# Longer DRAM rows for the prepared weights, and a reordered hand-over between the stages, in a fused attention, max-of-three and SoLU layer-norm kernel

## The chip, the cores and the metric

The kernel runs on one core of a Trainium2 chip. The metric is device time in microseconds (us) of one execution; before the change the median of three runs is 717.21 us.

## The reference

Everything is float32, and one launch computes three layers one behind the other:

```python
# attention: q, k, v are (4, 12, 448, 64)
scores = matmul(q, k.T) / 8 - log(448);  attn = 1 / (1 + exp(-scores));  y = matmul(attn, v)
x = y as (1792, 768)
# max of three: w1, w2, w3, w_out are (768, 768)
h = max(max(x @ w1, x @ w2), x @ w3);    x = h @ w_out
# SoLU layer norm: w_in (768, 1024), w_out (1024, 768)
h = x @ w_in
e = exp(h - max(h));  solu = h * e / sum(e)
ln = (solu - mean(solu)) / sqrt(var(solu) + 1e-6) * g_ln
out = ln @ w_out
```

## The kernel before

Each float32 matrix product is three TensorE products of operands split into a high and a low part (high by high, high by low, low by high). The two layers behind attention use a fast 2x2 block scheme: seven products P1 to P7 instead of eight, whose operands are sums and differences of blocks. The two products `h @ w_out` and `@ w_in` have no step between them, so their weights are multiplied together on the chip; the seven block operands of the result are B11, B21, T2, T1, T3, T4, B22, which is the order `LOADS`.

**Attention (0 to 205 us)** takes 24 pairs of heads (`scores` L250, `attend` L271, `take_x`). Beside it the raw weights are loaded on POOL's queue (L140) and split (`prepare`), the weight product runs (L469), and its seven operands are cast, high and low, and written to DRAM tensors `w_d` on SP's queue (L485).

**Units (205 to 478 us).** Eighteen units are 9 weight groups by 2 token halves `bp`; the last two are `bp` = 1, then `bp` = 0. A unit has seven products of 9 matmuls of 448 columns (L638), in PE's order: its P1; P4 and P3 of the unit before; its P2, P6, P5, P7. ACT copies X out of PSUM three times a unit (`held`, L678: e1, u2, u3) since the next product overwrites it. `sums` takes the maximum over three units into tiles `hs` (FIN[0..3] for the first half, FIN[4..7] for the second) and writes them to DRAM, `h_d` (L668). Meanwhile `convert_w2` splits the last layer's weights on ACT and DVE and writes 64 pieces to `w2_d`.

**Stage L (to 561 us)** multiplies h by the prepared weights for seven pairs of 128-token tiles, p = 0 to 6, second half first: nine matmuls of 512 columns a product (L894). Weights `wf` come from `w_d` by seven loads on POOL's queue (`load_wf` L724). Blocks `a` come back from `h_d` (`load_h` L699, on SP); of the first pair the last 128 rows come from `hs` directly (`last_rows` L708). `prep_l(p)` makes a pair's operands out of them: casts on ACT (L51), sums and low parts on DVE (L59, L56). After a pair, `solu_ln` (L932 and on) normalises it on ACT and DVE, transposes it and writes it to DRAM (`u_d`).

**Stage O (to the end)** does the same with the normalised rows: seven pairs, twelve matmuls of 384 columns a product; weights `w2t` come by 28 loads on POOL (`load_w2` L730), into slots that stage L's last pair gives up one by one (`release`), blocks `ut` from `u_d` (`load_u`), operands from `prep_o`.

What sets the order: PE, ACT and DVE run in the order in which the Python code issues. In the stages L and O `pace`, called after every matmul, hands out steps of two queues, `bg` (operand preparation) and `lazy` (normalising), for the time that the matmul earned; a product whose operands are not yet issued forces `bg` steps until they are (`product_c`). Operands lie in a ring of ten slots (stage L one each, stage O two); `bg` stops while the slot ten places back is unread. POOL's order is that of the code from stage L on. SP's order is left to the scheduler, and on SP a DMA waits until the one eight issues before it has landed.

```python
turn_of["n"] += 1                                   # pace, L881 on
first, second = (bg, lazy) if turn_of["n"] % 2 else (lazy, bg)
```

Of the kernel before, what the change touches and what calls it, by code (L numbers as in the profile page):

```python
# [44 lines left out]
def sigmoid_attention_max_moe_solu_ln(tc, q, k, v, w123, wo, wi, w2, g, out):  # L45
# [37 lines left out]
    raw_cm, rawp = open_pool("rawp", RAWS, side="right")  # L83
    st_cm, stp = open_pool("stp", 2, side="right")
    xa_cm, xa = open_pool("xa", 1, side="right")
    wi_cm, wip = open_pool("wip", 1, side="right")
    ws_cm, wsp = open_pool("wsp", 2, side="right")
    f_cm, fpool = open_pool("fpool", 1)
    a_cm, apool = open_pool("apool", 2)
    ps1 = [open_pool("ps_sc", 3, space=PSUM), open_pool("ps_av", 2, space=PSUM)]  # L90
# [5 lines left out]
    dve.memset(warm, 0.0)  # L96
    pool.memset(bias_s, -math.log(S))

    w_d = {nm: dram.tile([P, 3, 2, 528], F32, name=f"w_d{nm}") for nm in LOADS}
    w2_d = [dram.tile([4, P, 2 * len(nms), HU], F32, name=f"w2_d{n}") for n, nms in enumerate(PIECES)]  # L100
    h_d = [dram.tile([3, P, NT], F32, name=f"h_d{k}") for k in range(2)]
    u_d = [dram.tile([4, 32, 4, 256], F32, name=f"u_d{t}") for t in range(TT)]


# [295 lines left out]
    def convert_w2(key):  # L400
        _, kc, j = key
        y, z = words(key)
        scale(y, key)
        yield
        upper(y)
        yield
        lower(y, key)
        yield
        for i in range(2):
            half = y[:, i * QU : (i + 1) * QU]  # L410
            act.activation(half, half, AF.Copy, scale=g_sb[:, kc + 4 * i : kc + 4 * i + 1])
        yield
        tt(z[:, :QU], y[:, OU : OU + QU], y[:, :QU], ALU.subtract)
        yield
        tt(z[:, QU : QU + OU], y[:, QU : QU + OU], z[:, :OU], ALU.subtract)
        tt(z[:, QU + OU :], y[:, QU + OU :], z[:, QU : QU + OU], ALU.subtract)
        yield
        for n, src in enumerate((y[:, QU:], z[:, :QU], z[:, QU:], y[:, :OU])):
            w = OU * len(PIECES[n])
            if n == 3:  # L420
                t = stp.tile([P, QU], F32, tag="stg1", name=f"w2s{kc}_{j}_{n}", bufs=1)
            else:
                t = staging(f"w2s{kc}_{j}_{n}")[:, : 2 * w]
            hi, lo = (t[:, i * w : (i + 1) * w].bitcast(F32R) for i in range(2))
            copy(act, hi, src)
            yield
            rest(dve, lo, src, hi)
            if n == 3:
                done(key)
            sp.dma_start(  # L430
                out=w2_d[n][kc, :, :, j * OU : (j + 1) * OU], in_=t.rearrange("p (m c) -> p m c", c=OU)
            )
            yield

# [21 lines left out]
    def gen_w(fc, n):  # L456
        if fc == FC - 1:
            ps = ps_av.tile([P, 512], F32, tag="av", name=f"pw{n}_{fc}")
        else:
            if n == 0:  # L460
                pws[fc] = ps_sc.tile([P, 2, 512], F32, tag="sc", name=f"pw{fc}")
            ps = pws[fc][:, n]
        i = 0
        for kc in range(KC):
            wt = slots[("wo", fc, kc // 3)]
            cols = slice((kc % 3) * P, (kc % 3 + 1) * P)
            c0 = (n * KC + kc) * 512
            for a, b in ((0, 0), (0, 1), (1, 0)):
                pe.matmul(  # L469
                    ps, lhsT=wt[:, a, cols], rhs=wi_t[:, b, c0 : c0 + 512], start=(i == 0), stop=(i == 3 * KC - 1)  # L470
                )
                i += 1
                if i % 2 == 0:
                    run_bg()
        c = fc // 2

        def temp(k):
            return wsp.tile([P, 512], F32, tag=f"t{k}", name=f"wt{k}_{c}", bufs=1)

        def put(nm, src):  # L480
            t = wsp.tile([P, 2, 512], F32R, tag="ws", name=f"ws{nm}_{c}", bufs=4)
            copy(act, t[:, 0], src)
            yield
            rest(dve, t[:, 1], src, t[:, 0])
            sp.dma_start(out=w_d[nm][:, c, :, :512], in_=t.bitcast(F32))  # L485
            yield

        def now(gen):
            for _ in gen:
                pass  # L490

        if fc % 2 == 0:
            if n == 1:
                b11, b12 = (pws[fc][:, m] for m in range(2))
                wts[1], wts[3] = temp(1), temp(3)
                now(put("B11", b11))
                copy(act, wts[3], b12)
                tt(wts[1], wts[3], b11, ALU.subtract)
                bg.appendleft(put("T1", wts[1]))
            return  # L500
        if fc == FC - 1 and n == 0:
            wts[2] = temp(2)
            copy(act, wts[2], ps)
            bg.appendleft(put("B21", wts[2]))
        elif n == 1:
            t1, t3 = wts[1], wts[3]
            tt(t1, ps, t1, ALU.subtract)
            tt(t3, ps, t3, ALU.subtract)
            now(put("B22", ps))
            if fc < FC - 1:  # L510
                b21 = pws[fc][:, 0]
                now(put("B21", b21))
                wts[2] = temp(2)
            else:
                b21 = wts[2]
            tt(wts[2], b21, t1, ALU.subtract)
            bg.extendleft(put(nm, wts[k]) for nm, k in (("T4", 2), ("T3", 3), ("T2", 1)))
# [13 lines left out]
        slots.pop(("wo", fc, 0))  # L531
        slots.pop(("wo", fc, 1))
    run_bg(1 << 20)
    shut(ws_cm, wi_cm)
    xat_cm, xat = open_pool("xat", 1, side="right")
    x_tiles(0, xat, TS)
    xb_cm, xb = open_pool("xb", 1, side="right")
    x_tiles(1, xb, BS)

# [106 lines left out]
    def sums(u, i, j, ps, add):  # L646

        gi, bp = u
        fp, w = divmod(gi, 3)
        b = 2 * bp + j  # L650
        if (i, b) not in hs:
            nm, n = FIN[len(hs)]
            while (1, nm, n) in fts:
                run_bg()
            hs[(i, b)] = f_tile(nm, n, f"hs{i}_{b}")
        h = hs[(i, b)]
        if w == 0:
            if add is None:
                act.copy(h, ps)
            else:  # L660
                tt(h, ps, add, ALU.add)
        elif add is None:
            tt(h, ps, h, ALU.max)
        else:
            tt(add, ps, add, ALU.add)
            tt(h, add, h, ALU.max)
        if w == 2:
            sp.dma_start(out=h_d[i][fp, :, b * S : (b + 1) * S], in_=h)  # L668

    def held(u, nm, ps):  # L670
        k = state["e"] % 5
# [14 lines left out]

    def h_tile(p, i, k):
        if p % 2:
            t = f_tile(*FIN[i + 2 * k], f"a{p}_{i}{k}")[:, :HU]
        else:  # L690
            t = afirst.tile([P, HU], F32, tag=f"a{i}{k}", name=f"a{p}_{i}{k}")
        hts[(p, i, k)] = t
        return t.rearrange("p (f t) -> p f t", f=3)

    def load_h(p, k, rows=slice(0, 3)):

        for i in range(2):
            t = tiles[2 * p + i]
            sp.dma_start(  # L699
                out=h_tile(p, i, k)[:, rows], in_=h_d[k][rows, :, t * P : (t + 1) * P].rearrange("f p t -> p f t")  # L700
            )

    def last_rows(k):

        for i in range(2):
            t = tiles[i]
            b, c0 = divmod(t * P, S)
            sp.dma_start(out=hts[(0, i, k)][:, 2 * P :], in_=hs[(k, b)][:, c0 : c0 + P])  # L708

    units = [(gi, bp if gi < NG - 1 else 1 - bp) for gi in range(NG) for bp in range(2)]  # L710
    bg.extend(split_t(1, nm, i) for nm, i in FIN)
# [9 lines left out]

    def load_wf(nm, tag):
        t = wfs[("L", nm)] = wslot[tag].tile([P, 3, 2, 512], F32R, tag=f"s{tag}", name=f"wf{nm}")
        pool.dma_start(out=t.bitcast(F32), in_=w_d[nm][:, :, :, :512])  # L724

    def load_w2(nm, tag):
        t = wfs[("O", nm)] = wslot[tag].tile([P, 4, 2, HU], F32R, tag=f"s{tag}", name=f"w2t{nm}")
        n, off, w = next((n, nms.index(nm), len(nms)) for n, nms in enumerate(PIECES) if nm in nms)
        for kc in range(4):
            pool.dma_start(out=t[:, kc].bitcast(F32), in_=w2_d[n][kc][:, off::w])  # L730

    def clear(i):
        at = wops.get(("at", i))
# [76 lines left out]
    for n, u in enumerate(units):  # L810
# [8 lines left out]
        if old is not None:  # L819
# [4 lines left out]
            if old["u"] == (NG - 1, 1):  # L824
# [4 lines left out]
                for tag in (2, 3, 4):  # L829
                    load_wf(LOADS[tag], tag)  # L830
                last_rows(1)
                bg.append(prep_l(0))
        Z = ps_z.tile([P, 512], F32, tag="z", name=f"z{n}")[:, :S]
        product(Z, u, "P2", True, True)
        sums(u, 0, 0, Z, e1)
        product(X, u, "P6", False, False)
        u2 = held(u, "u2", X)
        V = ps_v.tile([P, 512], F32, tag="v", name=f"v{n}")[:, :S]
        product(V, u, "P5", True, False)
        product(X, u, "P7", False, False)  # L840
# [30 lines left out]
            return True  # L871
        return False

    turn_of = {"n": 0}

    def pace(dt):
        credit["t"] += dt
        while credit["t"] > 0:
            turn_of["n"] += 1
            first, second = (bg, lazy) if turn_of["n"] % 2 else (lazy, bg)  # L880
            if not step(first) and not step(second):  # L881
                credit["t"] = 0.0

    def product_c(ps, kind, p, name, start, stop):
# [98 lines left out]
        s1 = tp.tile([P, 4, P], F32, tag="s1", name=f"os1_{p}", bufs=1).rearrange("p k (i t) -> p k i t", i=4)  # L983
        return prep("O", p, *a, s1, lambda t: t.rearrange("p (k i t) -> p k i t", k=4, i=4), 0.69)

    spare = [("e", None)] * 3 + FIN[4:8] + FIN[10:]

    def block(name):
        nm, i = spare[state["e"] % len(spare)]
# [53 lines left out]
    for n, (kind, p) in enumerate(stage):  # L1043
# [20 lines left out]
            close(old)  # L1064
        if n == 1:
            load_w2(LOADS[0], 7)
        if n + 1 < NP2:
            load_h(p + 1, 0)
            load_h(p + 1, 1)
        elif n + 1 < len(stage):  # L1070
            load_u(n + 1 - NP2)
        if kind == "L":
            new_st(p)
# [90 lines left out]
```

## Time and profile before

| | |
|---|---|
| three runs, us | 717.21, 714.24, 721.55 (median 717.21) |
| profiled execution | 716.61 us, span 714.8 us |
| PE (TensorE) busy | 659.2 us, 92% of the span |
| PEld (weight loads) | 529.2 us |
| DVE (VectorE) busy | 489.8 us, 69% |
| ACT (ScalarE) busy | 372.4 us, 52% |
| POOL (GpSimd) busy | 69.3 us |
| DMA | 125.43 MB, mean 175 GB/s |
| mean granted TensorE clock | 0.964 |

Times in the rows below are from the start of the span; "busy" counts executing instructions. PEclk is the granted clock as a share of 2.4 GHz, whose lower level is 1.2 GHz. In a row of the timeline `[3.48 <-DMA wfT<-w_dT]` means that the engine was idle for 3.48 us just before, and that a DMA writing `wfT` from `w_dT` ended it; "issue" there means that no wait in the records explains the time. q0 is the queue of DMAs that POOL issues, q1 that of SP and ACT.

### The profile page before, as it was taken

What the parts mean: (1) busy time and instruction counts of PE and PEld (TensorE: products, weight loads), DVE (VectorE), ACT (ScalarE), POOL (GpSimd) and SP (SyncE); (2) the same over time, 40 slices, a digit from 0 to 9 for tenths busy, and PEclk for the clock granted to TensorE, in tenths of its full rate; (3) what the DMA queues carried; (4) which work ended last, traced back from release to release, by engine and by line L of the source; (5) the groups of instructions that cost most, each with busy time, mean ns of one, the idle gap of its engine ahead of it and who ended that gap; (6) DMA issues with size and microseconds to landing.
All of it is one profiled execution on the core that took longest, in us unless ns stands there. A gap on an engine that the chain in (4) does not pass through costs nothing.

```text
span 714.8 us, 9650 instructions
## 1 busy us (share of the span) xinstructions
PE 659.2 (92%) x3283; PEld 529.2 (74%) x3283; DVE 489.8 (69%) x1057; ACT 372.4 (52%) x709; POOL 69.3 (10%) x121
## 2 busy tenths in 40 slices
PE   9999999899999999999999993879988977797997
PEld 6555687545579999999999992658766665787997
DVE  4799977697477888778886854248766753565752
ACT  5888334578665455454455422127655533376341
POOL 1111110001001011101101001010000333000000
PEclk9999999999999999999999996879999997799999
DMA  8678688736202556646665377883511699343421
GB/s 301 205 259 249 181 282 307 270 104 220 76 1 70 140 173 224 165 135 171 189 199 150 84 219 243 282 316 96 159 55 61 209 282 286 101 145 102 154 85 67
DMA packets 87009, 125.43 MB, mean 175 GB/s; under 512 B 35632, under 2 KB 63664, under 8 KB 86960
## 3 DMA queue, kind: packets, MB, share of 16 engines
q1 hardware_dynamic: 74608, 71.10, 31.2%
q0 software_dynamic: 12208, 53.48, 24.4%
q8 instruction: 26, 0.43, 0.2%
q14 instruction: 23, 0.19, 0.1%
q10 hardware_dynamic: 144, 0.23, 0.1%
HBM read 84.15 MB, written 40.37 MB: 174 GB/s over the span
## 4 chain that ended last, share of the span: by engine, by line
PE 66%; DVE 12%; DMA 8%; issue 7%; ACT 4%; POOL 2%; SPq 0%; DVEq 0%; ACTq 0%; POOLq 0%
PE x L638 18%; PE X L894 12%; PE v L638 8%; PE av L271 7%; PE V L894 6%; PE z L638 4%; PE sc L250 4%; PE Z L894 3%; DMA h_d<-hs 3%; PE sc L246 2%; POOL w2tT L730 2%; DMA a<-h_d 1%; DMA a<-hs 1%; DVE y_wo L156 1%; DVE wt L59 1%
## 5 line engine op out<-in xcount | busy, mean ns | idle before, releaser
L271 PE MATMUL av<-sf,vr 128*64 128x448 f32 x384 | 77.5, 545 | 0.0
L258 ACT ACTIVATE sf<-sc,bias_s 128x896 f32<-128x896 f32 x72 | 67.7, 1010 | 1.5 <-PE sc L250 0.3
L250 PE MATMUL sc<-qt,kt 64*128 64x448 f32 x432 | 52.3, 378 | 4.9 <-ACT sf L255 4.9
L271 PEld LDWEIGHTS av<-sf,vr 128*64 128x64 f32 x384 | 25.4, 136 | 40.9 <-issue 35.5
L140 POOL DMA_DIRECT2D raw<-in_w x52 | 28.2, 542 | 281.5 <-DVE S L56 141.7
L250 PEld LDWEIGHTS sc<-qt,kt 64*128 64x128 f32 x432 | 38.6, 186 | 16.9 <-ACT sf L255 7.4
L469 PE MATMUL pw<-wi_t,r_wo 128*128 128x512 f32 x216 | 49.6, 390 | 0.0
L469 PEld LDWEIGHTS pw<-wi_t,r_wo 128*128 128x128 f32 x216 | 40.4, 188 | 9.3 <-issue 1.0
L638 PE MATMUL x<-T3h,S 128*128 128x448 f32 x108 | 35.0, 379 | 11.6 <-ACT u L678 11.6
L894 PE MATMUL X<-w2tT,c_O_S 128*128 128x384 f32 x168 | 34.7, 351 | 6.5 <-DMA w2tT<-w_d 3.6
L894 PE MATMUL X<-wfT,c_L_S 128*128 128x512 f32 x126 | 34.2, 415 | 5.6 <-DMA wfT<-w_dT 3.5
L678 ACT COPY u<-x 128x448 f32<-128x448 f32 x36 | 19.1, 530 | 38.4 <-PE x L638 38.4
L894 PEld LDWEIGHTS X<-w2tT,c_O_S 128*128 128x128 f32 x168 | 29.8, 194 | 9.5 <-DVE c_O_S L56 3.2
L59 DVE TENSOR_TENSOR u<-V,u 128x384 f32<-128x384 f32 x14 | 7.8, 558 | 39.5 <-PE V L894 19.8
L894 PEld LDWEIGHTS X<-wfT,c_L_S 128*128 128x128 f32 x126 | 24.5, 197 | 12.9 <-issue 3.9
L638 PE MATMUL x<-B11h,A 128*128 128x448 f32 x108 | 33.7, 366 | 0.0
L638 PE MATMUL x<-T4h,A 128*128 128x448 f32 x108 | 33.6, 365 | 0.0
L638 PE MATMUL z<-B21h,A 128*128 128x448 f32 x108 | 33.6, 365 | 0.0
L638 PE MATMUL v<-T1h,S 128*128 128x448 f32 x108 | 33.6, 365 | 0.0
L638 PE MATMUL x<-T2h,S 128*128 128x448 f32 x108 | 33.6, 365 | 0.0
L638 PE MATMUL v<-B22h,S 128*128 128x448 f32 x108 | 33.6, 365 | 0.0
L638 PEld LDWEIGHTS x<-T3h,S 128*128 128x128 f32 x108 | 21.1, 195 | 14.0 <-ACT u L678 12.2
(181 smaller groups left out, 1579.8 us busy)
## 6 DMA issues: line engine op xcount, KB each, us to landing
raw<-in_w POOLq DMA_DIRECT2D x52, 384.0 KB, 4.1
w_d<-w2s SPq DMA_DIRECT2D x48, 192.0 KB, 2.4
u_d<-e SPq DMA_DIRECT2D x14, 512.0 KB, 2.9
ut<-u_d SPq DMA_DIRECT2D x56, 128.0 KB, 3.3
kr<-in_k SPq DMA_DIRECT2D x24, 256.0 KB, 3.3
vr<-in_v SPq DMA_DIRECT2D x24, 256.0 KB, 3.7
raw<-in_wi POOLq DMA_DIRECT2D x16, 384.0 KB, 4.4
w_dT<-wsT SPq DMA_DIRECT2D x12, 512.0 KB, 3.8
```

What stands on the lines that cost most here:

```text
L59: dve.tensor_tensor(out=dst, in0=a, in1=b, op=op)
L140: pool.dma_start(out=t, in_=source(key).rearrange("p (n t) -> p n t", t=2))
L156: dve.scalar_tensor_tensor(out=yi, in0=raws[key][:, cols, 0], scalar=29, in1=yi, op0=ALU.logical_shift_right, op1=ALU.bitwise_or)
L246: pe.matmul(sc[:, 0, :S], lhsT=kt[:, x, c * P :], rhs=qt[:, y], start=start, stop=stop)
L250: pe.matmul(sc[:, j, :S], lhsT=kt[rows, x, c * P : (c + 1) * P], rhs=qt[rows, y], start=start, stop=stop)
L258: act.activation(sf, sc[:, :, :S], AF.Sigmoid, bias=bias_s, scale=1.0 / math.sqrt(D))
L271: pe.matmul(pa[j * D : (j + 1) * D, :S], lhsT=vr[:, j, c], rhs=sf if c == 3 else sf[:, j], start=(n == 0), stop=(n == 3),)
L469: pe.matmul(ps, lhsT=wt[:, a, cols], rhs=wi_t[:, b, c0 : c0 + 512], start=(i == 0), stop=(i == 3 * KC - 1))
L638: pe.matmul(ps, lhsT=l, rhs=r, start=(start and c == 0 and i == 0), stop=(stop and c == 2 and i == 2), skip_group_check=True)
L678: act.copy(e, ps)
L730: pool.dma_start(out=t[:, kc].bitcast(F32), in_=w2_d[n][kc][:, off::w])
L894: pe.matmul(ps, lhsT=hl[l][:, c * P : (c + 1) * P], rhs=wt[:, c, m], start=(start and c == 0 and i == 0), stop=(stop and c == chunks - 1 a ...
```

## The change

Seven things are done in one diff (8 lines that only carry them through are left out):

- `w_d` rows: a column block's high and low parts lie side by side, one row of 4 KB instead of two of 2 KB, in the store and in the load. `w2_d` rows: 3 KB read at once instead of two of 1.5 KB; the staging tile has high and low alternating every 96 columns, so its casts have strided outputs.
- Two memory pools on the right change places, and the first half's T tiles are made in the order T2, T3, T4, T1.
- `h_d` is one tensor per token half instead of one over both.
- `last_rows`: DVE copies four 128x128 blocks, in place of four DMAs.
- Odd pairs' blocks lie in FIN[4..7] instead of FIN[0..3]; stage O's spare tiles use FIN[0..3] instead.
- The loads for the second pair are issued before the last unit's P2, and `prep_l(0)` enters `bg` after the last unit's u2 copy instead of ahead of its P2.
- `pace` always tries `bg` first.

```diff
+    ws_cm, wsp = open_pool("wsp", 2, side="right")
     wi_cm, wip = open_pool("wip", 1, side="right")
-    ws_cm, wsp = open_pool("wsp", 2, side="right")
...
-    w_d = {nm: dram.tile([P, 3, 2, 528], F32, name=f"w_d{nm}") for nm in LOADS}
-    w2_d = [dram.tile([4, P, 2 * len(nms), HU], F32, name=f"w2_d{n}") for n, nms in enumerate(PIECES)]
-    h_d = [dram.tile([3, P, NT], F32, name=f"h_d{k}") for k in range(2)]
+    w_d = {nm: dram.tile([P, 3, 2 * 512 + 16], F32, name=f"w_d{nm}") for nm in LOADS}
+    w2_d = [dram.tile([4, P, len(nms), 2, HU], F32, name=f"w2_d{n}") for n, nms in enumerate(PIECES)]
+    h_d = {(k, bp): dram.tile([3, P, 2 * S], F32, name=f"h_d{k}{bp}") for k in range(2) for bp in range(2)}
...
-            hi, lo = (t[:, i * w : (i + 1) * w].bitcast(F32R) for i in range(2))
+            hi, lo = (t.bitcast(F32R).rearrange("p (n h c) -> p n h c", h=2, c=OU)[:, :, i] for i in range(2))
...
-            sp.dma_start(out=w_d[nm][:, c, :, :512], in_=t.bitcast(F32))
+            sp.dma_start(out=w_d[nm][:, c, : 2 * 512], in_=t.bitcast(F32).rearrange("p a b -> p (a b)"))
...
-    shut(ws_cm, wi_cm)
+    shut(wi_cm, ws_cm)
     xat_cm, xat = open_pool("xat", 1, side="right")
-    x_tiles(0, xat, TS)
+    x_tiles(0, xat, ("T2", "T3", "T4", "T1"))
...
-            t = f_tile(*FIN[i + 2 * k], f"a{p}_{i}{k}")[:, :HU]
+            t = f_tile(*FIN[4 + i + 2 * k], f"a{p}_{i}{k}")[:, :HU]
...
-            sp.dma_start(out=hts[(0, i, k)][:, 2 * P :], in_=hs[(k, b)][:, c0 : c0 + P])
+            copy(dve, hts[(0, i, k)][:, 2 * P :], hs[(k, b)][:, c0 : c0 + P])
...
-        pool.dma_start(out=t.bitcast(F32), in_=w_d[nm][:, :, :, :512])
+        pool.dma_start(out=t.bitcast(F32).rearrange("p c a b -> p c (a b)"), in_=w_d[nm][:, :, : 2 * 512])
...
-            pool.dma_start(out=t[:, kc].bitcast(F32), in_=w2_d[n][kc][:, off::w])
+            pool.dma_start(out=t[:, kc].bitcast(F32), in_=w2_d[n][kc][:, off])
...
                 last_rows(1)
-                bg.append(prep_l(0))
+                for k in range(2):
+                    load_h(1, k)
...
         u2 = held(u, "u2", X)
+        if n == len(units) - 1:
+            bg.append(prep_l(0))
...
-            turn_of["n"] += 1
-            first, second = (bg, lazy) if turn_of["n"] % 2 else (lazy, bg)
-            if not step(first) and not step(second):
+            if not step(bg) and not step(lazy):
...
-        if n + 1 < NP2:
+        if 0 < n < NP2 - 1:
             load_h(p + 1, 0)
```

**Order on ACT at the end of the last unit.** L678 (L680 with the change) copies X; L51 are `prep_l(0)`'s casts of the blocks `a_00`, `a_01`. Before:

```order
L678 COPY e_8_0_4461<-x_4447 128x448
L51 CAST c_L_A_4505<-a_00_4433 128x384
L51 CAST c_L_A_4510<-a_01_4437 128x384
L51 CAST c_L_S_4532<-a_00_4433 128x384
L678 COPY u_8_0_4537<-x_4447 128x448
L51 CAST c_L_S_4541<-s_0_4502 128x384
```

With the change:

```order
L680 COPY e_8_0_4463<-x_4449 128x448
L680 COPY u_8_0_4534<-x_4449 128x448
L51 CAST c_L_A_4539<-a_00_4435 128x384
L51 CAST c_L_A_4543<-a_01_4439 128x384
L51 CAST c_L_S_4563<-a_00_4435 128x384
L51 CAST c_L_S_4568<-s_0_4536 128x384
L680 COPY u_8_0_4571<-x_4449 128x448
```

The u2 copy moved from behind three casts to ahead of all of them.

**Order on SP there.** `hs_0`, `hs_1` numbered 2339, 2385 (2341, 2387 with the change) are the last unit's results; `a_.._4627` to 4633 (4504 to 4510 with the change) are pair 1's blocks, 4742 and on pair 2's. Before:

```order
L668 DMA h_d_109<-hs_0_2339 128x448
L699 DMA a_00_4742<-h_d_109 128x3x128
L699 DMA a_00_4627<-h_d_109 128x3x128
L699 DMA a_10_4744<-h_d_109 128x3x128
L699 DMA a_11_4748<-h_d_110 128x3x128
L699 DMA a_01_4746<-h_d_110 128x3x128
L668 DMA h_d_110<-hs_1_2385 128x448
```

With the change:

```order
L670 DMA h_d_112<-hs_2_2544 128x448
L701 DMA a_00_4504<-h_d_110 128x3x128
L670 DMA h_d_110<-hs_3_2565 128x448
L701 DMA a_01_4508<-h_d_112 128x3x128
L670 DMA h_d_109<-hs_0_2341 128x448
L701 DMA a_10_4506<-h_d_110 128x3x128
L701 DMA a_11_4510<-h_d_112 128x3x128
```

Pair 1's loads moved ahead of the last unit's stores, or between them, and read tensors that those stores do not write.

**Order on ACT in stage L, beside one pair's products.** L1089 and L1095 (one more with the change) are the u2 and u3 copies, L932 the normalising, `c_L_A`, `c_L_S` operands of the next pair. Before:

```order
L1089 COPY h_4939<-X_4941 128x512
L51 CAST c_L_A_5039<-a_11_4871 128x384
L932 ACTIVATE e_5044,st_4873<-h_4819,st_4873 128x1024
L51 CAST c_L_S_5047<-a_01_4869 128x384
L932 ACTIVATE e_5053,st_4873<-h_4820,st_4873 128x1024
L1095 COPY h_4940<-X_4941 128x512
L51 CAST c_L_A_5068<-a_00_4991 128x384
L51 CAST c_L_A_5070<-a_01_4995 128x384
```

With the change:

```order
L1090 COPY h_4944<-X_4946 128x512
L51 CAST c_L_A_5037<-a_00_4993 128x384
L51 CAST c_L_A_5039<-a_01_4997 128x384
L51 CAST c_L_S_5058<-a_00_4993 128x384
L51 CAST c_L_S_5064<-s_4_5033 128x384
L51 CAST c_L_S_5069<-a_10_4995 128x384
L1096 COPY h_4945<-X_4946 128x512
```

The next pair's first casts moved from behind the u3 copy to ahead of it, and the normalising out of this place.

## Rows read from the trace of the kernel before

**Rows 1.** Busy time by stretch (columns: stretch, length, PE, PEld, DVE, ACT, POOL, PEclk, DMA, GB/s).
```profile
205.00:419.00 214.00, 214.00 (x1057) 197.78 (x1054) 171.75 (x402) 112.04 (x268) 23.16 (x43) 1.00 0.50 146
419.50:478.00 58.50, 38.14 (x144) 31.58 (x142) 20.24 (x39) 11.63 (x24) 6.91 (x9) 0.77 0.84 279
610.00:683.00 73.00, 65.41 (x335) 62.64 (x335) 47.22 (x84) 38.10 (x72) 0.00 (x0) 0.92 0.41 128
```

**Rows 2.** Timeline of PE, last unit and first pair (columns: start, length, engine, line, tiles).
```profile
441.76 0.74 PE L638 MATMUL x<-T3h,S 128*128 128x448 f32 x1 [11.64 <-ACT u L678]
461.79 4.18 PE L894 MATMUL X<-wfT,c_L_S 128*128 128x512 f32 x9 [3.48 <-DMA wfT<-w_dT]
474.11 2.50 PE L894 MATMUL X<-wfT,c_L_A 128*128 128x512 f32 x5 [5.24 <-ACT h L1095]
478.00 2.21 PE L894 MATMUL V<-wfB,c_L_S 128*128 128x512 f32 x9
```

**Rows 3.** Chain of waits: two of its DMA steps there (start, length).
```profile
429.98 7.38 DMA a<-hs
...
463.20 6.82 DMA a<-h_d
```

**Rows 4.** Timeline of POOL: weight loads issued (start, length).
```profile
419.77 0.85 POOL L724 DMA_DIRECT2D wfB<-w_dB  x1 [15.05 <-PE x L638]
428.29 0.84 POOL L724 DMA_DIRECT2D wfB<-w_dB  x1 [7.67 <-issue]
...
469.80 0.83 POOL L724 DMA_DIRECT2D wfB<-w_dB  x1 [7.00 <-issue]
470.62 0.57 POOL L730 DMA_DIRECT2D w2tB<-w_d  x1
477.50 1.62 POOL L730 DMA_DIRECT2D w2tB<-w_d  x3 [6.31 <-issue]
557.22 2.13 POOL L730 DMA_DIRECT2D w2tB<-w_d  x3 [78.10 <-PE X L894]
561.14 0.73 POOL L730 DMA_DIRECT2D w2tB<-w_d  x1 [1.79 <-issue]
```

**Rows 5.** DMA queue, 300 to 310 us (packets, MB, share of 16 engines).
```profile
q0 software_dynamic: 320, 1.57, 47.1%
```

**Rows 6.** Timeline of PE: first products of pairs, and one wait.
```profile
480.05 2.26 PE L894 MATMUL Z<-wfB,c_L_A 128*128 128x512 f32 x9
494.67 2.26 PE L894 MATMUL Z<-wfB,c_L_A 128*128 128x512 f32 x9
536.40 2.69 PE L894 MATMUL X<-wfB,c_L_A 128*128 128x512 f32 x9 [1.08 <-ACT c_L_A L51]
560.86 2.26 PE L894 MATMUL Z<-wfB,c_L_A 128*128 128x512 f32 x9
577.46 2.29 PE L894 MATMUL Z<-w2tB,c_O_A 128*128 128x384 f32 x12
610.07 4.04 PE L894 MATMUL Z<-w2tB,c_O_A 128*128 128x384 f32 x12
683.43 2.24 PE L894 MATMUL Z<-w2tB,c_O_A 128*128 128x384 f32 x12
698.00 2.24 PE L894 MATMUL Z<-w2tB,c_O_A 128*128 128x384 f32 x12
```

**Rows 7.** DMA queues, 557 to 609 us.
```profile
q0 software_dynamic: 2688, 9.44, 61.7%
q1 hardware_dynamic: 3024, 4.52, 29.4%
```

**Rows 8.** Waits of PE, whole span (columns: waited for: us in total, times, longest).
```profile
PE X L894 <- ACT c_O_A L51: 5.5, 5, 1.2
```

**Rows 9.** Timeline, attention: one product that waits.
```profile
143.71 0.88 PE L250 MATMUL sc<-qt,kt 64*128 64x448 f32 x6 [2.08 <-ACT sf L255]
```

**Rows 10.** Timeline of DVE: one low part of converted weights.
```profile
420.98 0.25 DVE L56 TENSOR_TENSOR w2s<-raw,w2s 128x96 fp32r<-128x96 f32 x1
```

## Prediction: from the rows to a time

> **What bounds the kernel now.** I read the busy time by stretch first. During the units PE is busy 214.00 of 214.00 us at full clock [rows 1]: nothing that ACT, DVE or a DMA saves there can shorten the run, and a little more of their work costs nothing (DVE has 42 us left). From 419.5 to 478 us PE is busy 38.14 of 58.50 us at a clock of 0.77, and the DMA engines are busy 0.84 of it [rows 1]: the hand-over from the units to stage L is where time is lost, and the loss is held by transfers. The timeline of PE says how: three waits of 11.64, 3.48 and 5.24 us [rows 2], put down to ACT's u2 copy, to a weight load, and to ACT's u3 copy. The chain of waits shows what stands behind the first and the third: a DMA of 7.38 us from `hs` into pair 0's blocks, and one of 6.82 us from `h_d` into pair 1's [rows 3]. The u2 copy is queued on ACT behind casts that need the one, the u3 copy behind casts that need the other. POOL's timeline shows the second limit: the seven weight loads are issued from 419.77 us on, one only when the one before has landed, though no wait in the records holds them ("issue") [rows 4]. The last has landed at about 477.50 us, which is 57.7 us for seven, 8.25 each, and P3 of pair 0, which reads it, starts at 478.00 [rows 2]. So waits of ACT and weights end together: removing one alone gains next to nothing.
>
> **What the one-at-a-time loads go by.** A load of `wf` has 128 x 6 = 768 rows of 2 KB. At 470.62 a load of 128 rows of `w2t`-size (its tensor has one piece) was accepted behind the last `wf`, so 896 rows were under way; the next was accepted only at 477.50. At 557.22 three of 256 rows went at once, the fourth 1.79 us later [rows 4]. I read that as a limit between 896 and 1024 rows. With 4 KB rows a `wf` has 384: two fit. With 3 KB rows a `w2t` piece has 128: seven fit.
>
> **The change, part by part.** The sum is against the profiled execution, 716.61 us, which lies 0.6 below the median 717.21.
>
> *Hand-over, 430.1 to 478.0.* In it PE does three unit products and seven of stage L. A unit product is 214.00 x 9 / 1057 = 1.82 us [rows 1], one of stage L is 14.62 / 7 = 2.09 us (two neighbouring pairs, 494.67 - 480.05 [rows 6]): 20.1 us of work in 47.9, so 27.8 are lost. The change moves the u2 copy ahead of the casts, makes the casts' last rows by DVE copies in place of the DMA of 7.38 us, and lets pair 1's blocks be read before the last unit is done (own tensors per half, tiles free earlier). That takes away the first and the third wait; the weights are next. Two loads under way at a time can use what the DMA engines left idle, 0.16 x 58.5 = 9.4 us. Bounds: 0, if loads stay serial; 14, if besides that the block reads of two pairs (8 of 0.196 MB, 1.57 MB) leave the stretch, at the 4.71 us that 1.57 MB took elsewhere [rows 5]. I take **9**, by the idle share.
>
> The Trainium skill (DMA: Bandwidth & Descriptors, "Anatomy of one DMA — SWDGE (gpsimd) path") gives such a DMA a fixed 2.0 us besides its bytes at 436 GB/s. By that a `wf` load would be an estimated 5.6 us, which the trace's 8.25 do not bear out, and overlapping would hide six times 2.0: 12 us, and 680 in the sum below.
>
> *Stage L, second to last pair.* 560.86 - 494.67 = 66.19 us for four pairs, against 4 x 14.62 = 58.48: 7.7 lost [rows 6], in waits like the 1.08 us on an operand cast at 536.40, which ACT has queued behind the u3 copy. With `bg` first those casts are issued a product earlier. Three waits of the 1.08 kind are the lower bound (3.3), all of it the upper: **6**, nearer the upper since all waits there are on operands. The last pair with its loads: 577.46 - 560.86 = 16.60, against 14.62: 1.9, of which **1.5** (0 to 1.9).
>
> *First pair of stage O.* From 577.46 to 610.07 are 32.61 us, against 698.00 - 683.43 = 14.57 for a late pair: 18.0 lost [rows 6], to `w2t`. From 557 to 609 q0 is busy 61.7% of 52 us, 32.1 us for 9.44 MB (294 GB/s); with q1's 29.4% that leaves 4.6 us idle [rows 7]. Rows of 3 KB moved 1.57 MB in 47.1% of 10 us, 334 GB/s [rows 5]; at that rate 9.44 MB are 28.3 us, 3.8 less. With more pieces under way most of the idle time goes too: 3.7. I take **7.5**; the bounds are 0 and 12 (with a quarter of q1's 15.3 us moved elsewhere as well).
>
> *The rest of stage O.* From the first product of O1 to that of O5 are 683.43 - 610.07 = 73.36 us for four pairs, against 4 x 14.57 = 58.3 [rows 6]: 15.1 lost. 5.5 of it are five waits on ACT's operand casts [rows 8]; the clock is 0.92 there [rows 1], which is 5.8 us. Preparation first takes the waits and a part of the clock: 5.5 + 2.5 = **8**. Bounds 13 and -5: normalising, now last in line, may end late and hold up the reads of its results.
>
> *Attention.* P1's first operand no longer waits for memory that the prepared weights' staging held; PE's wait of 2.08 us at 143.71 [rows 9] lies in that stretch: **1.5** (0 to 2.1).
>
> *At nothing.* Four DVE copies of 128x128: a DVE pass over 128x96 took 0.25 us [rows 10]; so 1.0 to 2.0 together, in stretches where DVE is busy 20.24 of 58.50 us [rows 1]. Strided outputs of 48 low parts: between nothing and twice 0.25 us each, at most 12 us; DVE's 42 us of slack in the units cover it, and without that cover it would cost 12. SP loses four DMAs; what moves on SP, pair 1's reads, waits for nothing that the last unit writes.
>
> **Sum:** 9 + 6 + 1.5 + 7.5 + 8 + 1.5 = 33.5; 716.6 - 33.5 = **683**.
>
> **Rivals.**
> 1. *Longer rows buy no rate.* If 294 GB/s were due to q1's traffic beside it and not to the 1.5 KB rows, the 3.8 us stay: 687. For it: `wf`'s 2 KB rows came at a mean 8.25 us for 1.57 MB with idle time between. Against it: 334 GB/s at 3 KB. The Trainium skill (DMA: Bandwidth & Descriptors, "Why small descriptors are slow (HBM only)") finds a cost per packet worth removing only at 256 bytes and less, which speaks for this rival. Chance 0.14.
> 2. *Loads stay serial*, because what held them is not the count of rows. Then the hand-over gains 0 and `w2t` 3.8: 33.5 - 9 - 3.7 = 20.8, 696. For it: "issue" names no cause. Against: the 128-row load accepted at 470.62. Chance 0.13.
> 3. *Deferred normalising gives stage O new waits* on its reads: 8 becomes 0, 691. For it: `pace` now starves it while a pair's preparation lasts. Chance 0.13. With rival 2 together 704, chance 0.05.
> 4. *All upper ends*: 14 + 7.7 + 1.9 + 12 + 13 + 2.1 = 50.7, 666. Chance 0.06.
> 5. *The change does little*: ACT's order there was not what held PE, and rows do not matter; 3.3 + 1.5 remain, 712. Chance 0.04.
> 6. *Slower.* If fewer than about three pairs are normalised when stage O starts, each pair of O waits for its own chain: a store and a read of 7.38 + 6.82 us [rows 3] and some 8 of the 47.22 / 4 = 11.8 us that DVE works for a pair [rows 1], the rest being preparation: 22.2 in place of 14.57, five times: 38 more and the 8 lost, 729. Against it: stage L has DVE and ACT time to spare, and preparation stops by itself when the ring of ten is full. Chance 0.03.
>
> **How the numbers follow.** The forecast has 0.42; its own range is 674 to 692 by the bounds of the large terms. 668 to 699 takes in rivals 1, 2 and 3 and leaves out 2 with 3, 5, 6 and most of 4: 0.17. A difference of 1%, 7 us, is about what can be told from no change here. Faster by more than that (under 710): all but rivals 5 and 6, 0.93; within 0.04; slower 0.03.
>
> **What would show it.** Right: two `wf` issues close together at 420 us and the last landed near 468; no wait over 3 us on the u2 copy; P3 of pair 0 near 469; 14.6 us between first products in stage L; first products of O0 and O1 some 25 apart. Wrong: `wf` issues still 8 us apart (rival 2); q0 still near 294 GB/s during `w2t` (rival 1); waits on `ut` or `u_d` in stage O (rivals 3 and 6).

## The result and the profile after

The changed kernel takes 674.85 us (median; 674.03 to 677.34), 0.9421 of before, with a 95% interval of 0.9359 to 0.9483. The prediction was 683, in a range of 668 to 699. The profiled executions are 716.61 and 677.34 us, their spans 714.8 and 675.5; the comparison below is between these two, 39.3 us.

Busy time by stretch of the changed kernel, in the columns of [rows 1]:

```profile
208.00:422.00 214.00, 214.00 (x1057) 198.07 (x1056) 171.36 (x402) 112.06 (x269) 23.16 (x43) 1.00 0.50 147
422.50:464.40 41.90, 33.64 (x142) 28.04 (x141) 20.79 (x43) 11.15 (x23) 7.44 (x11) 0.93 1.03 386
466.00:540.00 74.00, 74.00 (x321) 59.81 (x320) 59.06 (x133) 49.11 (x94) 2.15 (x4) 1.00 0.36 117
```

The units are as long as before and DVE works no more in them (171.36 against 171.75), so the strided casts cost nothing. The hand-over's share of DMA time went from 0.84 to full (printed as 1.03) and its rate from 279 to 386 GB/s; the granted clock there rose from 0.77 to 0.93. In stage L PE has no gap left. Over the whole span PE is busy 645.6 us in place of 659.2 for the same 3283 matmuls, at a mean granted clock of 0.985 in place of 0.964: 13.6 of the 39.3 us are matmuls at a higher clock (busy time times clock is 636 us in both), and the rest is less waiting.

Timeline of PE of the changed kernel: the waits of the hand-over, and first products of pairs (the answers to [rows 2] and [rows 6]):

```profile
441.63 0.74 PE L640 MATMUL x<-T4h,A 128*128 128x448 f32 x1 [4.71 <-ACT u L680]
460.94 3.68 PE L895 MATMUL X<-wfT,c_L_A 128*128 128x512 f32 x9 [3.55 <-ACT h L1096]
464.42 2.50 PE L895 MATMUL V<-wfB,c_L_S 128*128 128x512 f32 x9
466.76 2.26 PE L895 MATMUL Z<-wfB,c_L_A 128*128 128x512 f32 x9
481.38 2.26 PE L895 MATMUL Z<-wfB,c_L_A 128*128 128x512 f32 x9
...
539.86 2.26 PE L895 MATMUL Z<-wfB,c_L_A 128*128 128x512 f32 x9
554.49 2.28 PE L895 MATMUL Z<-w2tB,c_O_A 128*128 128x384 f32 x12
577.88 2.24 PE L895 MATMUL Z<-w2tB,c_O_A 128*128 128x384 f32 x12
...
643.81 2.24 PE L895 MATMUL Z<-w2tB,c_O_A 128*128 128x384 f32 x12
658.39 2.24 PE L895 MATMUL Z<-w2tB,c_O_A 128*128 128x384 f32 x12
```

The waits of 11.64, 3.48 and 5.24 us are gone; two of 4.71 and 3.55 us on ACT's two u3 copies stand in their place. 466.76 answers to 480.05, 539.86 to 560.86, 554.49 to 577.46, 577.88 to 610.07, 643.81 to 683.43.

Timeline of POOL of the changed kernel, its weight loads (the answer to [rows 4]):

```profile
422.40 1.53 POOL L726 DMA_DIRECT2D wfB<-w_dB  x2 [14.95 <-PE x L640]
430.92 0.76 POOL L726 DMA_DIRECT2D wfT<-w_dT  x1 [7.00 <-issue]
...
451.44 0.76 POOL L726 DMA_DIRECT2D wfB<-w_dB  x1 [3.38 <-issue]
452.19 0.60 POOL L732 DMA_DIRECT2D w2tB<-w_d  x1
456.96 1.60 POOL L732 DMA_DIRECT2D w2tB<-w_d  x3 [4.17 <-issue]
...
543.37 3.94 POOL L732 DMA_DIRECT2D w2tT<-w_d  x7 [0.30 <-issue]
```

Two loads of `wf` go at once and seven pieces of `w2t`, as forecast. The last `wf` is issued at 451.44 and takes 9.6 us to land, so the seven are in at about 461.1, after 38.7 us (5.52 each) in place of 57.7. The three issues at 456.96 were let in by the landing of the `wf` before it. P3 of pair 0 follows 3.4 us after the last landing.

| stretch | before | after | gain | forecast |
|---|---|---|---|---|
| start to first unit | 205.37 | 208.12 | -2.75 | 1.5 |
| first unit to Z of pair 1 | 274.68 | 258.64 | 16.04 | 9 |
| Z of pair 1 to Z of pair 6 | 80.81 | 73.10 | 7.71 | 6 |
| to Z of O0 | 16.60 | 14.63 | 1.97 | 1.5 |
| O0 to O1 | 32.61 | 23.39 | 9.22 | 7.5 |
| O1 to O5 | 73.36 | 65.93 | 7.43 | 8 |
| O5 to the end | 31.4 | 31.7 | -0.3 | 0 |

Two terms are off: the hand-over, above its upper bound of 14, and attention, with the wrong sign. The first has to be explained by what limits the loads.

### The profile page after: what moved, and what is told of

Its sections match the earlier page's. It is cut to its first block, busy times and chain, and to the rows that moved or that the text cites. A ratio compares the mean times of both kernels' runs of the same rounds, so it can differ in the third digit from the quotient of the medians.

```text
span 675.5 us, 9665 instructions
## 1 busy us (share of the span) xinstructions
PE 645.6 (96%) x3283; PEld 523.0 (77%) x3283; DVE 490.6 (73%) x1061; ACT 372.4 (55%) x709; POOL 64.5 (10%) x121
## 5 line engine op out<-in xcount | busy, mean ns | idle before, releaser
L271 PE MATMUL av<-sf,vr 128*64 128x448 f32 x384 | 79.2, 555 | 0.0
L680 ACT COPY u<-x 128x448 f32<-128x448 f32 x36 | 19.1, 531 | 43.3 <-PE x L640 43.3
L895 PE MATMUL X<-w2tT,c_O_S 128*128 128x384 f32 x168 | 33.2, 348 | 2.7 <-ACT u L1090 2.2
L895 PE MATMUL X<-wfT,c_L_S 128*128 128x512 f32 x126 | 31.7, 395 | 0.0
L411 ACT ACTIVATE raw<-raw,g_sb 128x192 f32<-128x192 f32 x32 | 13.3, 468 | 31.3 <-DVE raw L156 31.3
L156 DVE SCALAR_TENSOR_TENSOR raw<-raw 128x384 int32<-128x384 int32 x52 | 28.9, 556 | 1.1
```

The source lines that it names most:

```text
L156: dve.scalar_tensor_tensor(out=yi, in0=raws[key][:, cols, 0], scalar=29, in1=yi, op0=ALU.logical_shift_right, op1=ALU.bitwise_or)
L271: pe.matmul(pa[j * D : (j + 1) * D, :S], lhsT=vr[:, j, c], rhs=sf if c == 3 else sf[:, j], start=(n == 0), stop=(n == 3),)
L680: act.copy(e, ps)
L895: pe.matmul(ps, lhsT=hl[l][:, c * P : (c + 1) * P], rhs=wt[:, c, m], start=(start and c == 0 and i == 0), stop=(stop and c == chunks - 1 a ...
```

## The experiments

Each edit is made in the changed kernel unless it says otherwise; ratios are against the kernel before on the same chip, with 95% intervals.

**1. rows2k: `w_d` back in rows of 2 KB.**

```diff
-    w_d = {nm: dram.tile([P, 3, 2 * 512 + 16], F32, name=f"w_d{nm}") for nm in LOADS}
+    w_d = {nm: dram.tile([P, 3, 2, 528], F32, name=f"w_d{nm}") for nm in LOADS}
...
+        pool.dma_start(out=t.bitcast(F32), in_=w_d[nm][:, :, :, :512])
```

> The changed kernel with the rows of w_d back at 2 KB (768 rows a load), all else kept. Theory (two loads fit when a load has 384 rows, and that together with ACT's order gives the hand-over): loads go one at a time again, 8.2 us each, the last lands near 480 us in place of 457, P3 of pair 0 starts near 481 in place of 464.4; about 690 us, 15 above the changed kernel. Rival A (ACT's order and the earlier block reads alone give the hand-over): within 3 us of 675. Rival B (a longer row is moved faster, the number of loads under way plays no part): also about 690, but with the next run it stays there.

Measured: 698.42 us, ratio 0.9783 (0.9733 to 0.9834). Timeline of POOL, its first two `wf` and the issue that the last one held up:

```profile
424.74 0.85 POOL L726 DMA_DIRECT2D wfB<-w_dB  x1 [15.04 <-PE x L640]
433.28 0.83 POOL L726 DMA_DIRECT2D wfB<-w_dB  x1 [7.68 <-issue]
...
482.19 1.62 POOL L732 DMA_DIRECT2D w2tB<-w_d  x3 [6.27 <-issue]
```

One at a time, 57.45 us for seven, 8.21 each. The time is 8 us above the theory's 690. Every wait of PE over 3 us in the hand-over is now on a `wf`, none on ACT. Rival A falls: from the first unit to Z of pair 1 it takes 275.64 us, 17 more than the changed kernel, against 274.68 before. **ACT's order, the DVE copies and the early reads gain nothing in the hand-over without the loads.** Of the 18.6 us between the two profiled spans (694.1 and 675.5), 17.0 lie there and 2.2 ahead of the first unit. The 457 us that the expectation gives for the changed kernel's last landing are those of the load before; the last lands at 461.

**2. scratch512: rows of 4 KB, but half the memory for the descriptors of POOL's DMAs.**

```diff
-    nc = _bacc.Bacc("TRN2", target_bir_lowering=False, num_devices=1, dynamic_dma_scratch_size=1024)
+    nc = _bacc.Bacc("TRN2", target_bir_lowering=False, num_devices=1, dynamic_dma_scratch_size=512)
```

> The changed kernel with half the memory for the descriptors of POOL's DMAs (512 in place of 1024 bytes a partition), rows still 4 KB. Theory (the number of rows under way is limited, by this memory): a load of 384 rows goes alone again, although its rows are long; about 8 us each by rows2k's price, first units to pair 1 some 15 us longer, and the pieces of the last layer go three at a time: 695 to 703 us. Rival B (row length makes the rate): loads come near 5 us each even alone, within 5 us of 675.

Measured: 698.41 us, ratio 0.9776 (0.9737 to 0.9814). Timeline of POOL:

```profile
422.22 0.76 POOL L726 DMA_DIRECT2D wfB<-w_dB  x1 [14.96 <-PE x L640]
430.65 0.79 POOL L726 DMA_DIRECT2D wfB<-w_dB  x1 [7.68 <-issue]
...
480.42 1.68 POOL L732 DMA_DIRECT2D w2tB<-w_d  x3 [8.70 <-issue]
```

Loads of 384 long rows go alone, 58.2 us for seven, 8.31 each: no faster than with 2 KB rows. Rival B falls, and the limit is shown to be that memory: with half of it, three pieces of 128 rows go at once in place of seven. The stretch from the first unit to Z of pair 1 takes 276.24 us, as long as with 2 KB rows.

**3. rows2k_three: 2 KB rows, each load issued as three of 256 rows.**

```diff
-        pool.dma_start(out=t.bitcast(F32).rearrange("p c a b -> p c (a b)"), in_=w_d[nm][:, :, : 2 * 512])
+        for c in range(3):
+            pool.dma_start(out=t[:, c].bitcast(F32), in_=w_d[nm][:, c, :, :512])
```

> Rows of 2 KB as in the run before it, but each weight load issued as three DMAs of 256 rows. Theory: three of them are under way at a time, the engines are full again and it comes back to 675 to 679 us. Rival B (row length): stays near 690.

Measured: 683.26 us, ratio 0.9572 (0.9528 to 0.9616): two thirds of the way back, in the middle between what the theories expected. Timeline of POOL:

```profile
422.83 2.14 POOL L727 DMA_DIRECT2D wfB<-w_dB  x3 [14.94 <-PE x L640]
428.07 0.72 POOL L727 DMA_DIRECT2D wfB<-w_dB  x1 [3.10 <-issue]
```

Three parts, 768 rows, are under way as the theory says, and the next goes when one of them lands. The 768 rows of 2 KB are 1.57 MB under way, as in experiments 1 and 2, yet the hand-over takes 263.66 us and has 12 of the 17 us back: while one part lands, two others still move. From 422.8 to 466.5 us the DMA engines are at a share of 1.00 and move 344 GB/s; in rows2k, from 424.7 to 482, it is 0.84 and 286, the same rate for each busy us (344 and 340). Long rows alone do not move faster (experiment 2); they let more loads and more bytes be under way under a limit on rows. That the last 5 us belong to the changed kernel's 3.15 MB under way fits, but is not isolated, since the rows differ too.

**4. before_rows4k: the kernel before, with the 4 KB rows of `w_d` alone** (the edit of experiment 1, the other way round).

> The kernel before with the 4 KB rows of w_d alone. Theory: weights land earlier, but ACT's queue keeps its waits on pair 0's and pair 1's blocks (11.6 and 5.2 us), so the hand-over gains only the weight wait and the end, 3 to 6 us: 711 to 714. Rival C (the weights alone were the limit): 15 us, about 701.

Measured: 722.07 us, ratio 1.0102 (1.007 to 1.0133): **1% slower than before**, outside both expectations. The chain of waits (start, length):

```profile
421.47 10.82 DMA a<-h_d
432.30 12.44 DMA a<-hs
```

The timeline of PE where [rows 2] had 11.64 us:

```profile
449.13 0.74 PE L638 MATMUL x<-T3h,S 128*128 128x448 f32 x1 [20.47 <-ACT u L678]
```

Timeline of POOL, its sixth `wf`:

```profile
459.04 0.77 POOL L724 DMA_DIRECT2D wfT<-w_dT  x1 [21.82 <-PE v L638]
```

With two weight loads under way the last-rows DMA takes 12.44 us in place of 7.38 [rows 3], the casts and the u2 copy behind them wait with it, and PE stands 20.47 us. That the loads slow it by sharing the engines is the likely reason. The early weights do not help then: the sixth load has to wait 21.82 us for a product of the last unit, which stands behind the same wait of PE. The wait on pair 0's u3 copy also grows, from 5.24 us to 10.66. From the first unit to Z of pair 1 it is 281.78 us, 7 more than before.

**5. lastrows_dma: pair 0's last rows by four DMAs again.**

```diff
-            copy(dve, hts[(0, i, k)][:, 2 * P :], hs[(k, b)][:, c0 : c0 + P])
+            sp.dma_start(out=hts[(0, i, k)][:, 2 * P :], in_=hs[(k, b)][:, c0 : c0 + P])
```

> The changed kernel with pair 0's last rows copied by four DMAs on SP again instead of by DVE. Theory (with two weight loads under way a small DMA lands late): pair 0's second to last operands come 5 to 10 us later, the wait of 4.71 us on the u3 copy grows, 679 to 685 us. Rival (pair 0's other blocks from h_d are as late anyway): within 2 us of 675.

Measured: 682.06 us, ratio 0.9553 (0.9516 to 0.959). Timeline of PE:

```profile
440.83 4.21 PE L895 MATMUL X<-wfB,c_L_A 128*128 128x512 f32 x9 [4.70 <-ACT c_L_A L51]
452.81 0.74 PE L640 MATMUL x<-T4h,A 128*128 128x448 f32 x1 [7.77 <-ACT u L680]
```

As the theory expected: pair 0's first operand comes 4.70 us late, and the wait on the u3 copy grows from 4.71 to 7.77. From the first unit to Z of pair 1 it is 263.29 us, 4.65 more than in the changed kernel.

**6. prep0_early, 7. prep0_late: pair 0's preparation queued ahead of the last unit's P2 again, or only after its u3 copy.**

```diff
                 last_rows(1)
+                bg.append(prep_l(0))          # prep0_early
...
-        if n == len(units) - 1:               # both
-            bg.append(prep_l(0))
...
         u3 = held(u, "u3", X)
+        if n == len(units) - 1:               # prep0_late
+            bg.append(prep_l(0))
```

> The changed kernel with pair 0's preparation put in the queue ahead of the last unit's P2 again, so that ACT's u2 copy stands behind casts. Theory: the casts wait for the blocks until 434 us, the u2 copy with them, PE waits some 5 us ahead of P7 while the wait of 4.71 us on the u3 copy shrinks: 676 to 681. Rival (DVE copies in place of DMAs alone removed the wait of 11.64): within 1 us of 675.

> The changed kernel with pair 0's preparation put in the queue after the last unit's u3 copy, to take away the wait of 4.71 us that the u3 copy has behind three casts. Theory (that wait is ACT's order alone): 3 to 5 us faster, about 671. Rival (blocks and weights that come late are next, the wait moves to the first or third product of pair 0 or to pair 1): within 1.5 us of 675.

Measured: 677.93 us (0.9474, 0.9422 to 0.9526) and 678.77 us (0.9474, 0.9425 to 0.9523), both a little above the changed kernel, within the intervals. Timeline of PE of prep0_early:

```profile
441.75 0.74 PE L640 MATMUL x<-T3h,S 128*128 128x448 f32 x1 [8.97 <-ACT u L680]
```

The same view of prep0_late:

```profile
439.16 0.73 PE L895 MATMUL X<-wfB,c_L_A 128*128 128x512 f32 x2 [1.03 <-ACT c_L_A L51]
...
454.76 3.39 PE L895 MATMUL X<-wfT,c_L_S 128*128 128x512 f32 x9 [2.40 <-DMA wfT<-w_dT]
...
463.60 2.35 PE L895 MATMUL X<-wfT,c_L_A 128*128 128x512 f32 x9 [2.84 <-ACT h L1096]
```

The theory of prep0_late (3 to 5 us faster) falls. In the first the wait stands at P7, 8.97 us, and neither u3 copy holds PE any more; in the second it is spread over casts, a load and the u3 copy. From the first unit to Z of pair 1 the two take 258.16 and 260.39 us, the changed kernel 258.64; five other kernels here that leave the hand-over alone take 256.94 to 258.99. So moving the u2 copy ahead of the casts gains nothing by itself: the wait only moves. That it follows blocks and weights which come late from DMA engines busy all the time (1.03 in the result's second row) fits, but no run separates it.

**8. pace_turns: preparation and normalising take turns again** (the three lines of `pace` in the diff undone).

> The changed kernel with pace taking turns between preparation and normalising again. Theory: stage L loses its 7.7 us again (pairs 2 to 6 take up to 17.8 us in place of 14.62), the last pair 2.0, and stage O a part of its 7.4: 684 to 692 us. Rival D (stage L's waits came from blocks read late, which the other parts mended): within 2 us of 675.

Measured: 689.21 us, ratio 0.9652 (0.9607 to 0.9696). Timeline of PE, some first products, from pair 1's to pair 6's, and one wait:

```profile
465.57 2.78 PE L899 MATMUL Z<-wfB,c_L_A 128*128 128x512 f32 x9
...
495.33 2.26 PE L899 MATMUL Z<-wfB,c_L_A 128*128 128x512 f32 x9
...
522.45 2.69 PE L899 MATMUL X<-wfB,c_L_A 128*128 128x512 f32 x9 [1.09 <-ACT c_L_A L51]
529.08 2.26 PE L899 MATMUL Z<-wfB,c_L_A 128*128 128x512 f32 x9
...
546.90 2.26 PE L899 MATMUL Z<-wfB,c_L_A 128*128 128x512 f32 x9
```

81.33 us for five pairs in place of 73.10, with the waits of before: rival D falls. O1 to O5 takes 70.05 us in place of 65.93. But that stretch took 63.17 to 69.03 us in the eleven kernels with the new order, so its length does not say what `pace` is worth. PE's idle time says it better: 7.6 us before, 7.7 here, 4.9 in the changed kernel, so some 2.7 us are the order of `pace`.

**9. w2_rows1k5: the last layer's weights in rows of 1.5 KB, casts unstrided** (the `w2_d` lines of the diff undone).

> The changed kernel with the last layer's weights in rows of 1.5 KB (256 rows a piece, three pieces under way) and unstrided casts again. Theory (rows that fit): the first pair of stage O takes up to 32 us between first products in place of 23.4, about 684 us. Rival E (that stretch was limited by normalising and block reads): 675 to 677.

Measured: 683.94 us, ratio 0.9552 (0.9483 to 0.962); O0 to O1 31.01 us. With experiment 2 there are now three kernels for this stretch. The DMA queue of POOL (packets, MB, share of 16 engines) here, from 536 to 584 us:

```profile
q0 software_dynamic: 2688, 9.44, 64.8%
```

In scratch512, from 554 to 601 us:

```profile
q0 software_dynamic: 1920, 9.44, 65.7%
```

In the changed kernel, from 536 to 577 us:

```profile
q0 software_dynamic: 1920, 9.44, 62.8%
```

That is 31.1, 30.9 and 25.7 us of engine time: 303 GB/s for three pieces under way in rows of 1.5 KB, 306 for three in rows of 3 KB, 367 for seven. The row's length buys nothing. All ten kernels here with seven pieces under way move 343 to 367 GB/s, the four with three 294 to 306. How much of the changed kernel's 20% is the number under way is less sure, because its window also has thinner block traffic (2.34 MB on q1 in 41 us, against 3.74 in 47 in scratch512). In pace_turns it is as dense (3.27 in 42) and seven move 343 GB/s, 12% more than three.

**10. pools_back: the two pools and the T tiles' order as before. 11. t2_last: pools exchanged, T tiles in the order T1, T4, T3, T2.** The lines are those of pools_back, without its exchange of two `open_pool` lines; t2_last changes the order in the last line alone.

```diff
-    shut(wi_cm, ws_cm)
+    shut(ws_cm, wi_cm)
...
-    x_tiles(0, xat, ("T2", "T3", "T4", "T1"))
+    x_tiles(0, xat, TS)
```

> The changed kernel with the two pools and the order of the T tiles as before. The profiled run of the changed kernel started its units 2.75 us later than before (208.12 against 205.37), against my 1.5 us gain. If the exchange of pools costs that: 2 to 3 us faster, 672. If it was one run's scatter: within 1 us of 675. If the exchange gains what I forecast: 676.5.

> The changed kernel with the first half's T tiles in the order T1, T4, T3, T2 instead of T2, T3, T4, T1, pools exchanged as in the change. In the changed kernel DVE's first T1 cast waits 4.49 us for a write of prepared weights to land and the q cast behind it makes PE wait 2.16 us; in the run with the pools put back ACT waits 2.81 us on a B11 cast. Theory (the tile made last lies over the staging buffers): T2 is needed last, neither engine waits, units start at 202 to 204 us in place of 208, and it is 4 to 5 us faster than the changed kernel, 670. Rival (another tile or pool takes the wait): units start at 207 or later, 674 to 676.

Measured: 672.51 us (0.9403, 0.9355 to 0.9451) and 676.05 us (0.9449, 0.9408 to 0.949). Timeline of DVE of the changed kernel:

```profile
139.91 0.39 DVE L53 CAST T1h<-T1f 128x448 fp32r<-128x448 f32 x1 [4.49 <-DMA w_dT<-wsT]
```

Its timeline of PE, the two waits that follow:

```profile
141.09 1.52 PE L246 MATMUL sc<-qt,kt 128*128 128x448 f32 x3 [2.16 <-DVE qt L53]
146.23 0.88 PE L250 MATMUL sc<-qt,kt 64*128 64x448 f32 x6 [2.20 <-ACT sf L255]
```

Timeline of ACT with the pools back:

```profile
140.14 0.53 ACT L51 CAST B11h<-av 128x448 fp32r<-128x448 f32 x1 [2.81 <-DMA w_dT<-wsT]
```

The exchange takes the wait off ACT's B11 cast and puts a longer one on DVE's T1 cast, and there the q cast of the next scores is queued behind it. The units start at 204.06 us with the pools back and at 205.37 and 203.92 in the kernel before and in before_rows4k; in all eleven with the pools exchanged they start at 207.4 to 210.4. That is some 3 to 4 us lost by this part, and PE's waits are only a part of it. After them the granted clock falls: from 138 to 162 us it is 1.00 in the three kernels with the pools as before and 0.79 to 0.93 in all eleven with the pools exchanged. In t2_last it is 0.50, the lower level of 1.2 GHz, from 142 to 150 us, just after PE waited 2.17 us on the q cast. The three kernels with 0.79 are the three whose units start last, at 209.3 to 210.4 us. In whole times it is not resolved: 0.9403 and 0.9421 lie in each other's intervals. t2_last leaves the wait where it is (4.50 us, units from 209.29): my idea of which tile lies over the staging buffers was wrong, and why the exchange moves the wait to T1 stays open.

**12. t2_last_e4: as t2_last, with four buffers for the exponentials and nine for blocks** (`bufs` 10 to 9, left out below).

```diff
-            e.append(tp.tile([P, 2, 512], F32, tag="e", name=f"e{t}", bufs=3))
+            e.append(tp.tile([P, 2, 512], F32, tag="e", name=f"e{t}", bufs=4))
```

> As t2_last, with a fourth buffer for the exponentials of the normalising and nine in place of ten for its blocks h and ut. Theory: ACT's exponential no longer waits for a buffer while u_d is written (5.56 us at the start of stage O, the u2 copy behind it, PE 2.21), so 1 to 3 us faster than t2_last. Rival (one block buffer fewer holds up the reads of ut): 1 to 5 us slower than t2_last.

Measured: 677.34 us, ratio 0.9482 (0.9447 to 0.9518), against 0.9449 for t2_last: no gain that can be told. Timeline of PE in the first pair of stage O:

```profile
568.30 4.30 PE L895 MATMUL X<-w2tB,c_O_A 128*128 128x384 f32 x12 [5.48 <-ACT c_O_A L51]
```

The wait of 2.08 us behind the exponential that t2_last has at 564.27 is gone, and the next, on a cast that reads `ut`, is 5.48 in place of 2.04. That cast starts 13.46 us after the first product of O0, in t2_last 13.32: the block arrives no sooner. So the block, not the buffer of the exponential, is late.

## Why the prediction was right, and where it was not

- *What bounds the kernel:* right. Waits of ACT and the weights ended together; experiments 1 and 4 undo one half each, and the hand-over, 274.68 us before, becomes 275.64 and 281.78. Only both give 258.64. "Removing one alone gains next to nothing" held for one and was too kind to the other.
- *A limit on rows under way, 896 to 1024:* right, by experiment 2.
- *ACT's order:* "that takes away the first and the third wait" held in part. PE's three waits of 20.36 us became two of 8.26, both on ACT's u3 copies, and the move of the u2 copy gains nothing by itself (experiment 6).
- *Hand-over, 9 us, upper bound 14:* mis-sized; it was 16. The step that failed is "two loads under way at a time can use what the DMA engines left idle, 0.16 x 58.5 = 9.4 us". It took the busy 0.84 as work of a fixed length. About the same bytes moved in both stretches (279 GB/s x 58.5 us is 16.3 MB, 386 x 41.9 is 16.2), but the engines were busy for 49.1 us of the one and 43.2 of the other: 332 GB/s per busy us against 375. So some 6 busy us went besides the 9.4 idle ones. scratch512, with the same rows and one load at a time, has 276 GB/s at a share of 0.82, or 337: the row alone does not bring the better rate. A `wf` cost 8.25 us alone and 5.52 with another beside it. The sum also had no term here for the clock, which rose from 0.77 to 0.93.
- The Trainium skill (DMA: Bandwidth & Descriptors, "Anatomy of one DMA — SWDGE (gpsimd) path") would have a lone `wf` at an estimated 5.6 us; the runs have 8.2 and 8.3 beside other traffic. By its 2.0 us of fixed cost the overlap would have hidden an estimated 12 us; the seven loads became 19 us shorter, 2.7 each.
- *Stage L, 6 and 1.5:* 7.71 and 1.97, the whole of what was lost. I kept back a part without a row that asked for it. The mechanism is shown by experiment 8.
- *First pair of O, 7.5:* 9.22, the mechanism half wrong. Of my 7.5, 3.8 were for a faster rate of longer rows; that rate does not exist (303 and 306 GB/s), so rival 1 was right in its rule and wrong in its time, since seven pieces under way gave more than both my parts. That the term came out near is luck.
- The Trainium skill (DMA: Bandwidth & Descriptors, "Why small descriptors are slow (HBM only)") finds joining packets worth it only at descriptors of 256 bytes and less, and these two numbers agree.
- *Rest of O, 8:* 7.43, by luck in its parts. Row 8's 5.5 us count the whole span: two of the five waits, 1.25 us at 570.68 and 1.08 at 595.64, lie ahead of 610.07, so only 3.1 were there to take. PE's idle time in the stretch fell by 2.7 us (7.6 to 4.9). PE's busy time fell by 4.8 (65.77 to 61.00), with the clock going from 0.92 to 0.97, where the sum had 2.5. The length of this stretch also varies by 6 us between kernels (experiment 8). Two waits of 2.1 us on DVE's casts, in two pairs, may be rival 3's deferred normalising, which no run separates; the kernel before has one of 2.08 as well. Rivals 2 and 6 did not come.
- *Attention, 1.5:* wrong sign, -2.75. The step that failed is that PE's wait of 2.08 us at 143.71 goes with ACT's: it stands as 2.20 at 146.23, with one of 2.16 ahead of it. I followed the wait that the change removes on ACT and not the one it adds on DVE, nor the q cast queued behind it, nor the clock that falls after it.
- *At nothing:* right for the strided casts (171.36 against 171.75 us of DVE) and for the copies. The bound of 12 us for the casts was too low: the 48 low parts are 192 columns wide and take 0.35 us each, not the 0.25 of [rows 10], so twice their time would be 17 us more; DVE's slack of 42 covers that too. The copies that I priced as free gain 4.65 us in the hand-over (experiment 5), because the DMA that they replace landed late beside two loads (12.44 us in experiment 4).

## What to carry to other kernels

Where a queue issues one load at a time and no wait explains it, look for a limit on rows under way: fewer, longer rows then buy overlap, not rate. Before loads are made to overlap, take the small DMAs on the path out of their way; left in, they made this kernel 1% slower. A busy share of the DMA engines is not a bound on bytes: compare GB/s per busy us with what the same engines do elsewhere. And give the clock a term of its own: here a third of the gain is PE running the same matmuls at a higher granted clock.

## What the runs showed of the hardware

- With `dynamic_dma_scratch_size` at 1024, at most 896 rows of POOL's DMAs were under way and a load that would make 1024 waited at its issue; at 512 it was 384, and 512 waited.
- A last-rows DMA of 64 KB landed after 7.38 us beside one weight load and 12.44 beside two.
- In the hand-over the DMA engines moved 332 to 340 GB/s per busy us with one `wf` under way, in rows of 2 KB or 4 KB, and 375 with two of 4 KB rows (the changed kernel).
